# A fused attention and mixer kernel: the hand-written order of all steps up to the last block is replaced by another

## The chip, the cores and the metric

The kernel runs on one core of a Trainium2 chip. A core has five engines that each take their own instructions in order: TensorE (PE in the profile, with PEld for its weight loads), VectorE (DVE), ScalarE (ACT), GpSimd (POOL) and SyncE (SP). They meet only at semaphores. DMA transfers are issued by SyncE, GpSimd and ScalarE and land later. The metric is the device time of one execution in microseconds (us).

## The reference

Causal attention over 8 batches of 8 heads, 576 tokens and head size 64, with 16 extra "beacon" keys that every token sees; then a token mixer of low rank and a two-layer channel network, both with a residual.

```python
k_all = np.concatenate([beacon_k, k], axis=2)
v_all = np.concatenate([beacon_v, v], axis=2)
scores = scale * np.matmul(q, k_all.transpose(0, 1, 3, 2))
scores = np.where(causal, -1000000000.0, scores)
...
a = np.exp(scores)
a /= a.sum(-1, keepdims=True) + 1e-09
x = np.matmul(a, v_all)        # (8, 8, 576, 64) -> (8, 576, 512)
...
h = xt @ U @ V                 # xt: x with its last two axes swapped, rank 32
u = x + h.transpose(0, 2, 1)
out = u + np.maximum(u @ w_ch1, 0.0) @ w_ch2     # 512 -> 2048 -> 512
```

## The kernel before

Attention works on 32 pairs of heads, four pairs to a batch (pair p is batch p // 4). The mixer's result is one row of 8 x 576 = 4,608 tokens, and the channel network takes it in nine blocks of 512. Blocks 0 to 5 start with plain products against w_ch1 (step g) and use a Strassen-like scheme of seven half-size products for w_ch2 (step P); blocks 6 to 8 use such a scheme for both (F and P).

What stands where is written out by hand. One string, SCRIPT (L855), lists 961 steps, and a loop runs them one after the other; a step puts its instructions at the end of the queue of each engine that it uses. No scheduler reorders them. So the string sets the order on every engine at once, and a letter in a step's name can choose the engine of a copy (V for DVE, A for ACT). The steps that matter here:

- q, k, b, v and w: loads, all issued by GpSimd. The k and q of a batch go into staging tiles st0 and st1 (512 KB each, the main part) and hd0 and hd1 (the first 64 or 80 tokens, "heads", and the beacons). st0, st1, hd0 and hd1 have two buffers each.
- G: regroups one pair's q or k from st into the tile pr, on DVE or ACT.
- R: turns pr into raw with a DMA transpose on SyncE (L283, `turn_pair`), from pair 12 on. The heads of q and k are turned straight into qT and kT (L276, `turn_heads`).
- T: brings one pair's q or k into qT or kT. For pairs 0 to 11 it transposes on PE (L261, L263, tile tps) and copies; from pair 12 on it copies from raw (L291 or L109).
- S: one visit of the scores. Sa, Sb, Sc and Sd take the four groups of key columns of a pair: 496, 464, 496 and 208 query columns (L316, tile sps). The two heads of the pair have 64 rows each and use the two halves of the array side by side; each gets a PSUM bank, and ACT takes the exp of each (L321, tile expt).
- M masks on DVE; A multiplies the scores by v on PE (L331, tile po) and normalises on DVE.
- x and X: the turn of the attention's result and the token mixer. X.0 (L371) uses 32 columns of the array at a time, X.1 and X.2 (L397) 32 rows.
- g, p, P, U, F, V, N, W: the channel network. g is four matmuls of 512 columns (L529, tile gps), evicted by ACT, and for the lower half of them by DVE too. P is eight matmuls of 256 columns per step (L620, tiles cpY, cpA, cpD). U turns a block's input on SyncE (tile ut). N makes sums of w_ch1 (wf0 to wf3), which the last three blocks use.
- I: an idle matmul of 512 columns on the whole array that keeps PE busy; `S..:n` issues n of them ahead of a visit.

PSUM has eight banks, handed out in the order of the steps. Two places of the code decide what a moved step brings with it. The heads of a batch are turned along with a pair unless a lower pair of the batch has been turned already:

```python
    def turn_of(p):
        b, c = divmod(p, NH2)
        if not any(b * NH2 + i in raw_of for i in range(c)):
            turn_heads(Ls[b], qT_of(b), kTs[b % 2], c)
        raw_of[p] = turn_pair(prs[p])
```

And the sums of w_ch1 live in the staging buffers of k and q (two of each), from the step that makes them to the end:

```python
                first_sums[j] = stage.tile([P, H, 4 * D], F16, name=f"wf{j}", tag=f"st{j % 2}").rearrange(
```

The last 21 steps of the string, from P83's neighbours on, and everything behind them (a general path that these inputs don't take) belong to no part of the change.

Of the kernel before, what the change touches and what calls it, by code (L numbers as in the profile page):

```python
# [27 lines left out]
def kernel(  # L28
# [762 lines left out]
    def step(t):  # L791
# [69 lines left out]
        TkA7 X0.0 X0.1 Sa5:0 X0.2 Sb4 TqV7 TqV6 Sc5 TkA6 v1A g0.9 Sc4 M4.1 Sb5 M5.1 U0.0 U0.2 g0.13
        GkV11 g0.1 M5.0 g0.10 g0.0 GkV8 g0.14 q2 g0.3 g0.11 GkA9 A5.0 A5.1 Sb7 I1 w11 TkV8 GqV8 GqV9 Sa7
        g0.2 M4.0 GqV11 Sd7 Sc7 TkV11 TkA9 g0.8 A4.1 M7.0 TqA9 A4.0 p00.0 p00.1 Sb6 v1B Sa6:0 g0.12
        p00.2 TqV11 M7.1 Sc6 g0.4 Sd6 g0.15 M6.0 GkA10 w20 U0.1 M6.1 TqV8 g0.6 A7.1 A7.0 Sd9 Sc9 w21
        A6.1 g0.7 A6.0 Sd8 g0.5 Sc8 Sa8 GqV10 X1.0 v2 b3 p01.0 p01.2 X1.1 P02.0 p01.1 X1.2 W0 P01.0 Sb8
        W4 W5 W1 Sb9 Sa9 W2 U1.1 W6 P01.1 TkA10 P02.1 M8.1 M9.0 TqA10 W7 b4 M8.0 U0.3 P05.0 P05.1 q3
        P06.0 P06.1 M9.1 A8.1 A9.0 A8.0 Sa10 P03.0 P03.1 k3 g1.15 A9.1 q4 Sa11 Sd10 g1.5 g1.1 Sb10 Sc10
        g1.3 g1.2 GkV13 GqA12 M10.0 GkA12 W3 P07.0 M10.1 P07.1 GqA13 Sb11 Sd11 GqA14 Sc11 M11.1 g1.9
        M11.0 GkA14 g1.12 A10.0 g1.7 g1.10 g1.0 R12 R13 R14 g1.6 TkV12 TqV12 TkV13 P04.0 GqA16 A11.1
        g1.8 U1.0 U1.3 TqA13 GkA15 P04.1 g1.14 A11.0 k4 A10.1 Sa13 Sd12 g1.11 p10.0 g1.4 GqA17 g1.13  # L870
        Sa12 Sb12 Sc12 p11.0 GqV15 X2.0 M12.0 P11.0 GkA17 P11.1 U1.2 X2.1 GkV16 p11.1 R15 P12.0 P12.1
        R16 P16.0 TqV14 Sd13 Sb13 M12.1 p10.1 p10.2 Sc13 P16.1 b5 U2.2 M13.0 TkA14 v3 A12.1 q5 A12.0 R17
        GkA19 P15.0 P15.1 p11.2 Sa14 Sd14 Sc14 x12 P17.0 TkV15 M13.1 P13.0 U2.3 A13.0 Sb14 Z16 M14.0
        P17.1 P13.1 GqA19 GqA18 TkV16 TqA16 A13.1 g2.13 g2.10 TqV17 TqV15 M14.1 v4 g2.4 Sa15 k5 Sc15
        TkA17 P14.0 A14.0 P14.1 A14.1 Sd16 GqV20 Sb15 Sd15 M15.1 GkV18 g2.0 x14 Sc16 M15.0 g2.7 g2.5
        g2.2 A15.0 A15.1 x13 Sd17 Sb17 g2.9 U2.0 X3.0 b6 Sa16 X2.2 g2.3 x15 Sa17 Sb16 R18 R19 Z18 GkV20
        M16.1 Sc17 M17.1 M17.0 g2.1 g2.6 g2.12 M16.0 g2.8 g2.15 A17.0 U2.1 TqA19 GqA21 TqA18 X3.1 A16.1
        A17.1 g2.14 A16.0 X3.2 g2.11 p21.0 P21.0 P21.1 GqA23 GkA21 q6 TkA18 p20.0 P22.0 P22.1 TkA19 R20
        p21.1 p20.1 Sc18 Sb18 P26.0 P26.1 R21 Sc19 Sd18 Sa19 p21.2 P25.0 P25.1 GkV22 p20.2 I1 Sd19 Sa18
        M18.0 U3.0 Sb19 M19.0 P27.0 M18.1 M19.1 P23.0 GqV24 GqA22 TqV20 P27.1 x16 P23.1 g3.11 TqA21  # L880
        GkV23 TkV20 TkA21 R22 b7 A19.1 g3.7 A19.0 R23 g3.13 g3.8 g3.5 Sa21 Sb21 Sc21 P24.0 P24.1 A18.1
        A18.0 Sb20 U3.3 Sd21 Sa20 M21.1 M21.0 g3.3 g3.2 Sc20 Sd20 X4.0 g3.4 M20.0 k6 GkV24 M20.1 g3.15
        GqA26 N5 v5 TkV22 g3.12 A21.0 U3.1 A20.0 g3.10 N1 GkA26 g3.1 x17 q7 g3.0 A20.1 TqV22 TqA23 TkV23
        g3.6 g3.14 g3.9 p30.0 p30.2 A21.1 Sc23 GkV25 p31.0 Sb23 GqV25 Sa23 R24 p30.1 x18 P31.0 P31.1
        GkV27 P32.0 P32.1 TkA24 p31.1 Sc22 p31.2 U3.2 k7 Sd22 v6 Sa22 P36.0 P36.1 Sb22 x19 M22.1 Sd23
        M23.0 P35.0 R25 R26 M22.0 P35.1 X4.1 P37.0 P37.1 X4.2 GqV27 TqA24 TqA25 P33.0 U4.1 P33.1 TkA25
        P34.0 R27 g4.0 GqV28 A22.1 TkV26 GkA28 R28 M23.1 g4.11 GqV29 g4.2 g4.6 TqV26 A23.0 g4.10 A23.1
        Sd25 Sc25 A22.0 g4.4 GkV29 R29 Sb25 GkV30 Sa25 M25.0 Sd24 TqV27 P34.1 TkA27 g4.3 U4.3 TkV28
        M25.1 g4.15 g4.13 g4.9 Sc24 Sa24 x21 Sb24 M24.0 U4.2 X5.0 A25.0 M24.1 g4.8 g4.12 U4.0 GqV31 x22
        g4.1 p40.0 p40.1 GqA30 A25.1 g4.7 Sa27 Sb27 A24.1 g4.14 A24.0 g4.5 p41.0 GkV31 Sc27 x23 Sc26  # L890
        p41.2 p41.1 Sd26 P41.0 P41.1 Sa26 Sd27 M27.1 Sb26 P45.0 p40.2 P42.0 P42.1 P45.1 TkA29 x20 X5.1
        U5.3 A27.1 R30 TqV29 M27.0 P46.0 P46.1 P43.0 P43.1 g5.13 A27.0 M26.0 M26.1 Sd29 g5.11 X5.2 g5.4
        U5.1 TqV28 P47.0 g5.2 A26.1 TkA30 x27 P47.1 A26.0 N0 Sb29 Sc29 R31 N4 g5.6 N2 Sb28 Sa29 g5.0 x24
        P44.0 g5.15 TqA30 M29.1 P44.1 x25 Sd28 Sa28 v7 Sc28 M28.1 M28.0 A29.1 g5.7 g5.14 TkV31 g5.1 g5.5
        M29.0 A28.0 g5.3 N3 A28.1 Sb30 TqV31 Sa30 g5.10 A29.0 U5.0 g5.12 g5.9 x29 g5.8 N6 p51.0 p51.2
# [5 lines left out]
        p61.0 V8.0 P61.0 V7.3 F64.2 F64.1 F76.0 F76.3 U7.1 p61.1 U6.3 p60.0 p60.1 p60.2 U6.0 P61.1 P62.0
        P62.1 P65.0 p61.2 P65.1 guard V7.2 P66.0 P66.1 P63.0 P63.1 F75.3 F72.0 F72.3 F75.2 F77.0 F73.0
        P67.0 P67.1 F73.3 F71.1 F71.2 F72.1 F72.2 F76.1 F76.2 F75.1 V8.2 V8.1 P64.0 P64.1 F77.1 F77.2
        V8.3 F81.0 F74.0 F73.1 F74.1 U8.2 F77.3 p70.0 p70.2 F74.2 sum F73.2 p71.0 P71.0 p70.1 F74.3
        p71.2 F85.1 p71.1 F81.1 P71.1 P72.0 P72.1 F85.3 P75.0 P75.1 P76.0 P76.1 P73.0 P73.1 F82.1 U8.1
# [125 lines left out]
```

## Time and profile before

| | us |
|---|---|
| median of 3 runs | 339.44 (338.67 to 341.15) |
| the profiled execution | 339.2 |
| its span, first to last instruction | 337.5 |

| engine | busy us | share of the span | instructions |
|---|---|---|---|
| PE | 327.8 | 97% | 3527 |
| PEld | 228.0 | 68% | 3527 |
| DVE | 264.8 | 78% | 690 |
| ACT | 228.0 | 68% | 494 |
| POOL | 99.3 | 29% | 129 |

The span of the profile is 1.7 us shorter than the time of the same execution. The granted TensorE clock was 0.998. A busy share is an average over stages: the start, where scores and loads come in (to about 34 us), the long middle where attention of one batch runs beside the channel network of another (to about 240 us), and the blocks at the end. Matmuls are pipelined and their ends are modelled, so PE's rate is read from start times that follow each other, and not from the duration of a row.

### The profile page before, as it was taken

The numbers are of one execution on the slowest core, as the hardware profiler recorded it, in microseconds if no ns is written. First come the engines' busy times: TensorE is split into PE (matmuls) and PEld (weight loads), VectorE is DVE, ScalarE is ACT, GpSimd is POOL, SyncE is SP. The second block draws the span as 40 slices with busy tenths as digits, with TensorE's granted clock in tenths as the row PEclk, the third lists the DMA queues.
The fourth block names the chain that finished last, engine by engine and source line by source line (L and its number), as shares of the span: only waits on it lengthen the run. The fifth ranks groups of instructions, "written<-read, shape, count | busy, mean of one in ns | idle before, by whom it ended". The sixth has DMA issues, their size and how long they took to land.

```text
span 337.5 us, 8954 instructions
## 1 busy us (share of the span) xinstructions
PE 327.8 (97%) x3527; PEld 228.0 (68%) x3527; DVE 264.8 (78%) x690; ACT 228.0 (68%) x494; POOL 99.3 (29%) x129
## 2 busy tenths in 40 slices
...
GB/s 178 221 196 196 153 167 195 98 168 175 164 180 176 169 188 150 124 136 187 189 109 145 172 183 96 83 114 100 51 62 161 93 2 63 80 0 95 3 113 98
DMA packets 136145, 44.17 MB, mean 131 GB/s; under 512 B 108417, under 2 KB 131969, under 8 KB 136097
## 3 DMA queue, kind: packets, MB, share of 16 engines
q0 software_dynamic: 69008, 17.54, 61.3%
q1 hardware_dynamic: 66496, 25.66, 42.0%
...
q10 hardware_dynamic: 592, 0.34, 0.3%
...
## 4 chain that ended last, share of the span: by engine, by line
PE 75%; DVE 16%; DMA 3%; issue 3%; ACT 2%; SPq 0%; DVEq 0%; ACTq 0%
PE gps L529 23%; PE cpY L620 15%; PE po L331 8%; PE sps L316 8%; PE cpD L620 7%; PE cpA L620 3%; PE fpY L566 3%; DMA stm<-in_q_dram 3%; DVE gT L581 3%; DVE sT L601 2%; DVE ob L645 2%; DVE uT L404 2%; PE fpD L566 2%; PE tps L263 1%; ACT expt L321 1%
## 5 line engine op out<-in xcount | busy, mean ns | idle before, releaser
L321 ACT ACTIVATE expt<-sps 128x496 f16<-128x496 f32 (+2 forms) x256 | 111.6, 538 | 15.8 <-PE sps L316 14.3
L529 PE MATMUL gps<-uT,w 128*128 128x512 f16 x384 | 91.8, 379 | 0.0
L620 PEld LDWEIGHTS <-gT 128*128 128x128 f16 x576 | 54.6, 98 | 10.5 <-issue 2.2
L529 PEld LDWEIGHTS <-w 128*128 128x128 f16 x384 | 34.3, 98 | 37.4 <-issue 2.5
L587 POOL TENSOR_SCALAR gT<-gT 128x512 f16<-128x512 f16 x12 | 17.8, 1495 | 105.6 <-DVE gT L581 89.0
L620 PEld LDWEIGHTS <-sT 128*128 128x128 f16 x432 | 41.0, 98 | 7.8 <-issue 2.0
L331 PEld LDWEIGHTS <-expt 128*128 128x128 f16 (+1 forms) x960 | 35.5, 98 | 9.2 <-DVE expt L304 1.3
L203 POOL DMA_DIRECT2D vs<-in_v_dram x50 | 40.5, 825 | 3.2 <-DMA w<-in_moe_w_ch_dram 2.5
L539 ACT ACTIVATE gT<-gps 128x512 f16<-128x512 f32 x48 | 29.8, 630 | 15.5 <-PE gps L529 15.2
L304 DVE TENSOR_TENSOR expt<-expt,bigmask 128x512 f16<-128x512 f16 x64 | 26.7, 417 | 17.2 <-ACT expt L321 17.2
L331 PE MATMUL po<-vs,expt 128*128 128x65 f16 (+1 forms) x960 | 38.0, 194 | 1.0 <-ACT expt L321 1.0
L620 PE MATMUL cpY<-wsum,gT 128*128 128x256 f16 x288 | 36.1, 273 | 0.0
L620 PE MATMUL cpD<-w,sT 128*128 128x256 f16 x288 | 35.5, 273 | 0.3 <-DVE sT L601 0.3
L316 PE MATMUL sps<-qT,kT 64*128 64x80 f16 (+4 forms) x384 | 34.5, 282 | 0.4 <-ACT kT L109 0.3
L340 DVE TENSOR_TENSOR xb<-po,rec 128x320 f16<-128x320 f32 x64 | 31.5, 492 | 2.2
L534 DVE SCALAR_TENSOR_TENSOR gT<-gps,gT 128x256 f16<-128x256 f32 x48 | 19.8, 420 | 14.9 <-ACT gT L533 14.8
L109 ACT ACTIVATE hP<-fpY 128x512 f32<-128x512 f32 x24 | 13.7, 598 | 23.0 <-PE fpY L566 18.8
L533 ACT ACTIVATE gT<-gps 128x256 f16<-128x256 f32 x48 | 19.5, 418 | 11.5 <-PE gps L529 11.0
L316 PEld LDWEIGHTS <-kT 64*128 64x128 f16 x384 | 13.9, 94 | 18.7 <-issue 10.1
L645 DVE TENSOR_TENSOR ob<-cpY,ut 128x512 f32<-128x512 f32 (+1 forms) x28 | 18.7, 667 | 6.0 <-PE cpY L620 6.0
L566 PEld LDWEIGHTS <-wf 128*128 128x128 f16 x192 | 18.6, 98 | 3.0 <-issue 0.7
L620 PE MATMUL cpY<-w,gT 128*128 128x256 f16 x144 | 17.7, 273 | 0.0
...
## 6 DMA issues: line engine op xcount, KB each, us to landing
out_dram<-ob SPq DMA_DIRECT2D x16, 512.0 KB, 4.5
st<-in_k_dram POOLq DMA_DIRECT2D x6, 512.0 KB, 8.9
st<-in_q_dram POOLq DMA_DIRECT2D x6, 512.0 KB, 8.6
...
w<-in_moe_w_ch_dram POOLq DMA_DIRECT2D x4, 512.0 KB, 8.6
...
```

The costliest lines, as they stand in the source:

```text
L203: nc.gpsimd.dma_start(out=dst[a : a + nq[j], j, :, :], in_=src[hs, ds(q0[j], nq[j]), :].rearrange("h p d -> p h d"))
L304: nc.vector.tensor_tensor(out=e4, in0=e4, in1=bigmask, op=ALU.min)
L316: nc.tensor.matmul(ps[i][:, ds(o, w)], kT[hp, c, ds(P * ch, P)], qT[hp, c, ds(qa, w)], start=True, stop=True,)
L321: nc.scalar.activation(out=ex[i][:, ds(PAD + SLOT * g, gw[g])], in_=ps[i][:, 0 : gw[g]], func=AF.Exp, scale=scale)
L331: nc.tensor.matmul(po[:, j, :], ex[0 : nk[c], ds(blk[(c, j)], P)], vs[0 : nk[c], ds(c * H * E + h * E, E)], start=(c == 0), stop=(c == j),)
L340: nc.vector.tensor_tensor(out=xb[:, h // 2, :, ds(D * (h % 2), D)], in0=po[:, :, 0:D], in1=r.broadcast_to([P, NT, D]), op=ALU.mult)
L529: nc.tensor.matmul(g, w1[:, cc, ts(dc, P)], uT[:, cc, ds(ring(t0), 512)], start=(cc == 0), stop=(cc == NCC - 1))
L534: nc.vector.scalar_tensor_tensor(out=gT[:, dc, H2:512], in0=g[:, H2:512], scalar=0.0, in1=gT[:, dc, 0:H2], op0=ALU.max, op1=ALU.subtract,)
L539: nc.scalar.activation(out=gT[:, dc, :], in_=g, func=AF.Relu)
L566: nc.tensor.matmul(ps[:, i, :], a[:, kk, ts(2 * mp + i, P)], b[:, kk, :], start=opens and i == 0 and kk == 0, stop=kk == 1, skip_group_che ...
L620: nc.tensor.matmul(ps[:, i, :], a[:, f, ds(P * i, P)], b[:, f, :], start=opens and i == 0 and f == 0, stop=f == NK - 1, skip_group_check=True,
L645: nc.vector.tensor_tensor(out=out, in0=ps[:, ii, :], in1=other, op=ALU.add)
```

## The change

The string is replaced by another with the same 961 steps. Up to the last 21 the order differs; 61 steps of copying (H, G, T, e) also change their engine, in both directions. The loads keep their order among each other. The number of instructions on PE and of idle matmuls stays the same.

```diff
     SCRIPT = """
-        HqA0 I1 GkA0 I1 I1 I1 GqA0 I1 I1 HkV0 u I1 I1 I1 GkV1 I1 B I1 I1 I1 TqA0 TkA0 I1 TkV1 I1 s v0A
+        I1 I1 I1 GkV1 I1 I1 I1 HqA0 I1 HkA0 I1 GqA0 I1 I1 I1 I1 I1 v0A GkA0 v0B TqV0 TkV0 TkV1 I1 I1 Sa0:3
...
```

Three places show it. On PE, the score visits of pairs 8 and 9 beside the products of block 0. Here sps are scores (128x208 is visit d, 128x336 the first part of visit c), po is attention times v, gps is a product of block 0, and qtp is the mixer. Before:

```order
L331 MATMUL po_1268<-vs1_127,expt0_120 128x65
L316 LDWEIGHTS kT0_124
L316 MATMUL sps0_1286<-qT_989,kT0_124 128x208
L316 LDWEIGHTS kT0_124
L316 MATMUL sps1_1287<-qT_989,kT0_124 128x208
L529 LDWEIGHTS w1_108
L529 MATMUL gps_1292<-uT_118,w1_108 128x512
```

After:

```order
L371 MATMUL qtp_1279<-xb_934,Usb_111 32x128
L316 LDWEIGHTS kT0_124
L316 MATMUL sps0_1302<-qT_1036,kT0_124 128x208
L316 LDWEIGHTS kT0_124
L316 MATMUL sps1_1303<-qT_1036,kT0_124 128x208
L316 LDWEIGHTS kT0_124
L316 MATMUL sps0_1308<-qT_1036,kT0_124 128x336
```

Before, visit d of pair 8 stands alone between two groups of full-array matmuls; after, visit d of pair 9 is followed by visit c of pair 8 at once (and that by visit b of pair 9), and ahead of it stands a group of the mixer that uses a part of the array too. Over the program there are 68 unbroken stretches of score matmuls before and 56 after. Visits in one stretch number three in 21 of the stretches before and in 26 after.

On SyncE, the turns of batch 3 (hd1 and hd0 are its heads, raw its pairs; ut is a block's input, ob a result on its way out). Before:

```order
L650 DMA out_0_dram<-ob_1449 128x2x512
L276 DMA_TRANSPOSE qT_1800<-hd1_1346 128x4x64
L276 DMA_TRANSPOSE kT1_125<-hd0_1345 128x4x80
L283 DMA_TRANSPOSE raw_1803<-pr_1695 128x8x128
L283 DMA_TRANSPOSE raw_1805<-pr_1693 128x8x128
L283 DMA_TRANSPOSE raw_1807<-pr_1733 128x8x128
L520 DMA_TRANSPOSE ut_1438<-uT_118 128x4x128 x2
```

After:

```order
L276 DMA_TRANSPOSE qT_1721<-hd1_1349 128x2x64
L276 DMA_TRANSPOSE kT1_125<-hd0_1348 128x2x80
L283 DMA_TRANSPOSE raw_1724<-pr_1498 128x8x128
L276 DMA_TRANSPOSE qT_1721<-hd1_1349 128x3x64
L276 DMA_TRANSPOSE kT1_125<-hd0_1348 128x3x80
L283 DMA_TRANSPOSE raw_1760<-pr_1638 128x8x128
L276 DMA_TRANSPOSE qT_1721<-hd1_1349 128x4x64
L276 DMA_TRANSPOSE kT1_125<-hd0_1348 128x4x80
L283 DMA_TRANSPOSE raw_1779<-pr_1500 128x8x128
L650 DMA out_0_dram<-ob_1419 128x2x512
L520 DMA_TRANSPOSE ut_1439<-uT_118 128x4x128 x3
```

Pairs 12, 13, 14 were turned in rising order, with the heads once; now it is 14, 13, 12, each with the heads of its own and all higher pairs again. In the other batches pairs 17 and 16, 22 and 20, 25 and 24 change places like that, so head turns go from 10 to 20.

On DVE, the first sum of w_ch1 (wf0) and the copies from k's staging tile (st0; st0_1423 is batch 4's, st0_2556 batch 6's, st1_1424 is q's). Before:

```order
L253 COPY pr_2956<-st0_2556 128x512
L304 TENSOR_TENSOR expt1_121<-expt1_121,bigmask_107 128x4x128
L306 TENSOR_TENSOR expt1_121<-expt1_121,mask_102 80x80
L489 TENSOR_TENSOR wf0_3236<-w1_108 128x1024
L291 COPY kT1_125<-raw_2991 128x512
```

After:

```order
L645 TENSOR_TENSOR ob_1973<-cpD_2076,ob_1973 128x2x256
L489 TENSOR_TENSOR wf0_2228<-w1_108 128x1024
L534 SCALAR_TENSOR_TENSOR gT_2230<-gps_2231,gT_2230 128x256
L253 COPY pr_2238<-st1_1424 128x512
L645 TENSOR_TENSOR ob_1974<-cpY_1904,ob_1974 128x2x256
L304 TENSOR_TENSOR expt3_123<-expt3_123,bigmask_107 128x4x128
L306 TENSOR_TENSOR expt3_123<-expt3_123,mask_102 80x80
L253 COPY pr_2238<-st0_1423 128x512
```

The first sum moved from a place among batch 6's copies to one among batch 4's, so it takes one of k's two staging buffers two batches sooner.

More of the change, by code (lines that the diff above doesn't have):

```diff
@@ L861 @@
[L861 to L895, printed above, removed]
@@ L901 @@
[L901 to L905, printed above, removed]
@@ new lines @@
+        w12 A0.1 GqV3 I1 Sa1:2 b1 Sc1 I1 M1.1 A0.0 I1 TkV3 Sb2 Sc2 M1.0 GqV5 I1 I1 A1.1 TqV3 GqA4 Sd2 Sa2:1
+        I1 k1B I1 TqA5 I1 GkV5 A1.0 q1B Sb3 Sc3 I1 TqA4 M2.1 Sd3 Sa3:1 cV w13 A2.1 GkV4 b2 I1 I1 w10 M2.0
+        TkV4 k2 TkA5 A2.0 GkA7 I1 M3.1 I1 I1 v1A Sa4 Sb4 Sd4 M3.0 GqV6 A3.1 A3.0 eV I1 GkV6 Sa5:0 X0.0 Sd5
+        X0.2 Sc4 TqV6 GqA7 X0.1 Sc5 Sb5 M5.1 M4.0 GkV10 TkA7 TkV6 U0.2 M5.0 U0.1 g0.15 M4.1 q2 g0.11 TqV7
+        g0.3 w11 g0.0 U0.3 g0.8 g0.10 A4.0 A4.1 v1B Sa6:0 Sc6 A5.1 g0.2 GkA9 GqV10 GqV8 Sd6 Sb6 GqV9 TkA10
@@ new lines @@
+        w20 A5.0 M6.1 M6.0 GkV8 TkV9 U0.0 g0.1 g0.9 Sa7 Sc7 p00.0 g0.14 g0.12 TqA9 TqV8 TkV8 TqV10 g0.6 Sb7
+        Sd7 w21 g0.13 M7.1 M7.0 A6.0 g0.4 A7.1 GkA11 A7.0 A6.1 GqV11 g0.7 g0.5 X1.0 Sd9 Sc8 Sb9 p00.2 TkV11
+        v2 P01.0 b3 p01.0 p01.1 X1.1 X1.2 Sc9 p00.1 P01.1 b4 W0 W4 q3 P02.0 U1.2 Sa8 Sd8 W1 W5 W2 W6 P02.1
+        Sa9 Sb8 TqA11 P05.0 k3 p01.2 GqA14 GqA12 P05.1 M9.1 P06.0 P06.1 P03.0 P03.1 M9.0 M8.1 P07.0 q4 g1.0
+        W7 A9.0 k4 A8.1 g1.1 g1.2 M8.0 g1.11 g1.13 GkV13 P07.1 GkV14 W3 A8.0 A9.1 Sb11 Sd11 GqV13 g1.8 g1.3
@@ new lines @@
+        P04.0 R14 Sa10 Sc11 Sc10 g1.12 R13 GkV12 g1.4 g1.5 R12 g1.6 P04.1 g1.7 Sd10 Sa11 Sb10 M11.0 M11.1
+        g1.14 GqA16 M10.1 g1.10 TqA14 M10.0 TkA12 TqV13 A11.0 g1.9 U1.1 g1.15 b5 A10.1 p10.0 P11.0 A11.1
+        U1.0 GkV17 U1.3 TqA12 TkA14 v3 A10.0 GqA15 TkV13 p11.0 P11.1 GkV16 Sb12 Sc12 GqA17 R17 q5 Sa12
+        p10.1 p11.1 P12.0 P12.1 P16.0 Sd12 Sd13 X2.0 R16 M12.1 P15.0 M12.0 p11.2 p10.2 P16.1 Sc13 Sa13 Sb13
+        P15.1 GkV15 P17.0 M13.0 R15 X2.1 P13.0 A12.1 A12.0 U2.1 P13.1 N1 g2.0 GqV19 Sa14 Sb14 Sc14 TqA16
@@ new lines @@
+        U2.3 P17.1 TqA15 Z16 g2.12 g2.14 M13.1 GkV19 g2.1 g2.2 A13.0 TkA15 A13.1 TkV17 g2.7 Sd14 Sc15 GqA22
+        P14.0 Sd15 Sb15 Sa15 M14.1 GkV18 g2.11 M14.0 M15.1 R19 P14.1 v4 U2.0 g2.6 A14.0 k5 TqV17 g2.4 M15.0
+        A14.1 GqA18 x14 TkA16 b6 x12 g2.13 g2.5 g2.10 g2.15 GkV20 A15.1 Sd16 Sc16 Sb16 g2.9 A15.0 GkV22 R18
+        TqV19 U2.2 g2.8 g2.3 X2.2 X3.0 p21.0 x13 Sb17 Sa16 Sa17 p20.0 p20.1 GqV20 P21.0 Z18 q6 p21.1 P21.1
+        Sc17 Sd17 p20.2 TqA18 x15 M17.0 P22.0 GkV21 P25.0 TkA19 R22 M16.1 X3.2 R20 TkA18 p21.2 P25.1 P26.0
@@ new lines @@
+        P22.1 P26.1 b7 X3.1 A16.1 GqA21 R21 P23.0 P27.0 M16.0 P23.1 M17.1 g3.15 A17.0 GkA23 A16.0 Sc18 Sb18
+        Sa18 k6 v5 P27.1 g3.1 TkA20 TkV22 A17.1 TqA22 TkV21 Sd18 M18.1 GqV24 Sc19 M18.0 P24.0 g3.12 g3.6
+        GqV23 P24.1 TqA20 Sd19 Sa19 Sb19 A18.1 g3.10 GqV25 GkV24 A18.0 TqA21 M19.0 g3.9 g3.2 M19.1 R23 Sc20
+        GkA25 U3.1 N2 Sa20 Sd20 g3.5 g3.13 A19.0 g3.3 U3.3 A19.1 Sb20 Sd21 R25 M20.1 g3.7 M20.0 U3.0 TqV23
+        TkV23 x19 Sb21 Sa21 Sc21 M21.0 GqA27 GkV27 g3.8 A20.1 A20.0 g3.11 x16 M21.1 g3.0 g3.14 p30.0 x17
@@ new lines @@
+        g3.4 p31.0 Sb22 Sc22 X4.0 GqV26 p30.1 U3.2 A21.1 P31.0 P31.1 x18 A21.0 p30.2 p31.1 R24 Sa22 Sc23
+        Sd23 P36.0 P36.1 q7 Sd22 Sa23 Sb23 P35.0 M22.1 GkV26 R27 p31.2 P35.1 X4.2 M22.0 k7 M23.0 TkA24
+        P32.0 TqV25 P33.0 P37.0 X4.1 TkV25 M23.1 P32.1 R26 P33.1 v6 N5 A22.0 TqV24 g4.8 A23.0 g4.14 A23.1
+        g4.15 g4.1 P37.1 g4.11 A22.1 Sb24 Sa24 Sd25 P34.0 P34.1 GkV28 Sd24 Sb25 X5.0 Sc25 Sc24 Sa25 TkV26
+        M24.1 g4.13 GkV29 M25.0 g4.5 TkA27 U4.0 M25.1 g4.12 GqV28 M24.0 g4.10 U4.2 g4.6 g4.0 g4.9 g4.4
```

32 lines of the change are left out of this document (20 added, 12 removed).

## The prediction

> **What bounds the kernel now.** I read the busy time by stage first, then TensorE's waits, and then its instructions in order of time. The columns of the first are each engine's busy us in a stretch, with instruction counts.
>
> ```profile
> core 0: us, PE busy (x) PEld busy (x) DVE busy (x) ACT busy (x) POOL busy (x), PEclk, DMA share, GB/s
> 0.00:34.00 34.00, 29.85 (x354) 16.40 (x355) 24.35 (x103) 26.13 (x65) 24.42 (x43) 1.00 1.38 198
> 34.00:240.00 206.00, 205.96 (x2259) 132.10 (x2261) 159.03 (x432) 163.96 (x358) 57.03 (x74) 1.00 1.34 148
> 240.00:280.00 40.00, 39.66 (x451) 33.68 (x451) 38.54 (x84) 18.52 (x38) 6.05 (x4) 1.00 0.43 78
> 280.00:337.50 57.50, 52.33 (x474) 45.83 (x471) 42.89 (x74) 19.36 (x35) 11.75 (x8) 0.99 0.22 66
> PE idle L241 <- POOL ident masks.py:199: 1.6, 1, 1.6
> PE po L331 <- ACT expt L321: 1.0, 1, 1.0
> ```
>
> From 34 to 240 us TensorE (PE) has 205.96 busy us in 206.00: it waits for nobody there. VectorE (DVE) and ScalarE (ACT) are busy 77% and 80% of it. Only 240 to 280 has a second full engine, DVE with 38.54 of 40. So the order can change the time in two ways: PE's own work can get shorter, or a wait can be put in where now there is none. The removable waits are small: outside the 1.6 us at the very start the longest is 1.0.
>
> A busy PE is not yet a PE at its peak, so the second look is at start times of PE rows that follow each other.
>
> ```profile
> 143.48 0.38 PE L241 MATMUL idle<-ident 128*128 128x512 f16 x1
> 143.79 0.70 PE L316 MATMUL sps<-qT,kT 64*128 64x208 f16 x6
> 144.43 1.05 PE L620 MATMUL cpY<-wsum,gT 128*128 128x256 f16 x8
> 145.31 1.04 PE L620 MATMUL cpD<-w,sT 128*128 128x256 f16 x8
> ...
> 147.93 1.03 PE L529 MATMUL gps<-uT,w 128*128 128x512 f16 x4
> 148.79 0.63 PE L331 MATMUL po<-vs,expt 128*128 128x65 f16 x15
> 149.26 1.03 PE L529 MATMUL gps<-uT,w 128*128 128x512 f16 x4
> ...
> 204.26 1.03 PE L529 MATMUL gps<-uT,w 128*128 128x512 f16 x4
> 205.22 0.69 PE L316 MATMUL sps<-qT,kT 64*128 64x336 f16 x14
> ```
>
> Four gps matmuls followed by po, also a full-array matmul, take 148.79 - 147.93 = 0.86 us from start to start, 0.42 ns a column. The same four followed by a score (64 rows of the array, "64*128") take 205.22 - 204.26 = 0.96. **Entering a score stretch costs 0.10 us.** Leaving: the six score matmuls at 143.79 are three visits of 208, 496 and 464 columns, two heads side by side, so 1,168 columns or 0.49 us, and cpY starts 0.64 later. The 0.15 left over holds the exit and two steps from visit to visit; I take 0.10 for an exit, like an entry.
>
> **The change, part by part.**
>
> *Score stretches.* By the built order the 3,527 matmuls change the part of the array in use 177 times before and 148 after: score stretches go from 68 to 56 (24 changes), and the groups on 32 rows or columns now more often stand next to a score (5 more). 29 x 0.10 = 2.9 us, all on PE and so on the path. Bounds: 29 x 0.095 (entry seen behind the idle matmul: 0.31 us to the next start, less 0.215 for 512 columns) = 2.75, and 29 x 0.15 = 4.3 if the whole left-over belonged to the exit. I take 2.9; two clean entries stand behind it.
>
> The Trainium skill, TensorEngine Tiling (Array Packing), Key Properties, says that a change of tiling mode drains the engine. TensorE: Matmul & The Clock Gate, Step-by-step, puts a drain at about 128 cycles; at one column a cycle and the row's 0.42 ns that is an estimated 0.054 us, and the sum would be 1.6 us and not 2.9. The row shows more, and the row decides.
>
> *Idle matmuls.* The same 44 are issued (37 in steps of their own). Before, two stand behind the first gps row, one of them at 143.48; after, none does. Each holds a full PE for 0.215 us: -0.4. In the start they fill waits and cost nothing as long as those waits exist; without that cover they cost the 0.4 again.
>
> *Engines of copies.* Six copies from raw move from DVE to ACT, and others move back.
>
> ```profile
> L109 ACT ACTIVATE kT<-raw 128x512 f16<-128x512 f16 x10 | 11.2, 1128 | 0.0
> L109 ACT ACTIVATE pr<-st 128x512 f16<-128x512 f16 x24 | 15.0, 646 | 1.5 <-DMA raw<-pr 1.5
> L291 DVE COPY kT<-raw 128x512 f16<-128x512 f16 x10 | 6.1, 608 | 1.0 <-DMA raw<-pr 1.0
> L321 ACT ACTIVATE expt<-sps 128x496 f16<-128x496 f32 (+2 forms) x256 | 111.6, 538 | 15.8 <-PE sps L316 14.3
> ```
>
> ACT: +6 x 1.12, -6 x 0.63 (pr), and smaller ones, between +1 and +2 us of 228; DVE about even. PE hides it: ACT has 42 us free between 34 and 240. What is not hidden is a burst. An exp takes 111.6 / 256 = 0.44 us, so a stretch of three visits gives ACT 2.6 us of work in 0.6 us of PE. Before there are 21 such stretches, after 26; the 21 leave no PE wait in the rows from 34 to 240. I take 0.3 us; ends 0 and 3 (one PE wait of 0.6 for each of the five more).
>
> *Start.* qT and kT of pair 0 move from ACT to DVE, behind the copy of pair 1's k.
>
> ```profile
> 6.93 0.49 DVE L253 CAST pr<-stm 128x512 f16<-128x512 f32 x1 [0.83 <-DMA stm<-in_k_dram]
> 7.81 0.73 ACT L109 ACTIVATE kT<-tps 128x80 f16<-128x80 f16 x2
> 8.08 0.20 DVE L264 COPY kT<-tps 128x80 f16<-128x80 f16 x1
> 8.19 0.68 DVE L265 COPY kT<-tps 128x512 f16<-128x512 f16 x1
> 8.60 0.46 PE L316 MATMUL sps<-qT,kT 64*128 64x208 f16 x4 [0.34 <-ACT kT L109]
> 34.19 1.02 PE L529 MATMUL gps<-uT,w 128*128 128x512 f16 x4
> ```
>
> DVE is free of that copy at 7.42 and of its head copy (0.20) at 7.6; two times 0.78 (8.08 to 8.87) end at 9.2, so the first score starts near 9.2 and not at 8.60: +0.6. Later DVE has about 1.2 us more before the mix of batch 0. Against that PE gets all scores of pairs 4 and 5 done before the first gps, and PE is idle 34.00 - 29.85 = 4.15 us there, 1.6 of them before its first instruction, so 2.5 could still be won. Ends -2.5 and +1.8; I take +0.3, nearer to the later first score, which is certain.
>
> *SyncE.* Heads (L276) are now turned again for each pair that goes ahead of a lower one of its batch: ten issues become twenty, and each later one waits until the earlier one into the same tile has landed.
>
> ```profile
> L276 SPq DMA_TRANSPOSE qT<-hd x5: 1175/1185/1299, 74.3 to 187.4; - x5
> L276 SPq DMA_TRANSPOSE kT<-hd x5: 1186/1211/1292, 76.3 to 188.7; - x5
> DMA to landing us min/median/max: 2.3/7.3/10.3
> L283 SPq DMA_TRANSPOSE raw<-pr x20: 1232/1338/5233, 79.8 to 221.0; - x20
> raw<-pr SPq DMA_TRANSPOSE x20, 4.6
> ACT pr L109 <- DMA raw<-pr: 1.5, 1, 1.5
> POOL hd L193 <- PE tps L263: 8.7, 1, 8.7
> 33.37 31.16 SPq L520 DMA_TRANSPOSE ut<-uT  x5
> 73.75 0.41 SPq L650 DMA_DIRECT2D out_dram<-ob  x1
> ```
>
> Ten issues are 12 us more of SyncE's queue, and the outputs and the turns of ut and xt stand behind them. The worst place is pairs 14, 13, 12. From the first head turn to raw of pair 12 landed, before: 2 x 1.2 + 3 x 1.34 + 4.6 = 11 us. After: two rounds in which kT's turn is issued 1.2 behind qT's and then has to land, then 2.4, one raw and its landing, 2 x (1.2 + 7.3) + 2.4 + 1.3 + 4.6 = 25 at the median landing and 15 at the shortest. Behind the ACT copy that waits for it PE still has two g (0.86 each), two products (0.88 each, 144.43 to 145.31) and three po groups (0.47 each, 148.79 to 149.26), 4.9 us, before it needs ACT. The copies from raw wait 1.5 and 1.0 us at most now (ACT's above, DVE's in the copies' rows). The heads' loads stood 8.7 us behind the last transposes of batch 2, which for k now come some 7 us of PE work sooner, so fewer loads should be under way when the heads are turned. I take the shortest landing, 4 us more, which the 4.9 cover: 0.2 us. Ends 0 and 14 - 4.9 = 9.
>
> *Loads.* The four st buffers are two for k and two for q, and a sum of w1 (wf0) takes one of k's for good as soon as it is made. Before, that is behind k's load of batch 6; after, it is ahead of batch 5's, so k of batches 5 to 7 uses one buffer, and each load starts when the last copy of the batch before is done.
>
> ```profile
> POOL st L196 <- DVE pr L253: 24.4, 1, 24.4
> st<-in_k_dram POOLq DMA_DIRECT2D x6, 512.0 KB, 8.9
> ```
>
> Before, GpSimd waits like that once, for batch 7, and nobody on PE's side waits for it. After, 7.8 us of PE work stand between the last copy of batch 4's k and the first of batch 5's, 9.5 for batch 6, against 0.9 to issue and 8.9 to land: DVE is held up to 2.0 and 0.3 us, with GpSimd's later loads queued behind. PE's banks cover most of it: +0.5; ends 0 and 2.3.
>
> **Sum**, against the profiled execution (339.2; span 337.5 and 1.7 around it): -2.9 - 0.4 + 0.3 (bursts) + 0.3 (start) + 0.2 (turns) + 0.5 (loads) = -2.0, so 337.2. The median of the runs, 339.44, lies 0.2 above that execution: **337.4**. About 1% is what a measurement can tell from no change: 336.0 and 342.8.
>
> **Rivals.** (a) The start is won too: the first gps row comes 1.5 us sooner and the new waits are all covered: 339.4 - 2.9 - 0.4 - 1.5 + 0.4 = 335.0. For it: 2.5 idle us, and more scores ahead of the first gps; against it: the first score is later and DVE has more before the mix.
>
> (b) The repeated head turns hold ACT at pairs 14 to 12: with landings at the median 7.3, 14 us later than now, less 4 of lead (SyncE issues nothing from 64.5 to 73.75 and could run ahead by part of that) and 4.9 of cover, PE stands 5: 339.4 - 2.0 + 5 = 342.4, slower than before. It decides from a landing of 4.6 us on. For it: the median of 7.3; against it: the shortest of 2.3, and the sooner loads.
>
> (c) Banks: visits of a stretch take two of eight PSUM banks each, and PE stands behind the exps. At 0.6 us on each of the five added stretches of three it gives 3: 339.4 - 2.0 + 2.7 = 340.1. The Trainium skill, Perfetto Trace Analysis, Matmuls, asks that independent groups rotate through the banks so that evacuation overlaps the next matmuls; that speaks for this rival. Against it: the 21 stretches of three in the rows now.
>
> (d) The stretches save nothing, because the 0.10 would come back as waits of the same length for ACT: 339.4. The two entries, one behind gps and one behind an idle matmul that waits for nobody, speak against.
>
> **Chances.** The forecast 0.52, within 336.0 and 339.0; (a) 0.20; (b) 0.14; (c) 0.09; (d) 0.05. Range 334.8 to 341.6: it leaves out the far side of (a) and most of (b). Faster by over 1%: (a) and the edge of the forecast, 0.24. Slower by over 1%: the upper half of (b), 0.07. Within: 0.69.
>
> **What would show it.** Right: between 34 and 240 us the PE rows keep no idle time while the last gps rows come 2 to 3 us sooner; fewer, longer score rows; GpSimd waiting for pr at three k loads; L276 x10 each. Wrong: a wait of PE for ACT or DVE of over 2 us near 85 to 100 us (turns) or near 120 and 150 (loads); ACT waiting for raw by more than 5 us; a first gps row that has moved by more than 2 us either way.

## The result: 1.4% slower

The new kernel takes 343.55 us in the median of 4 runs (341.88 to 346.85), the one before 339.14: a ratio of 1.0141, with a 95% interval of 1.0097 to 1.0186. Forecast were 337.4, with 334.8 to 341.6. The profiled execution took 344.79 us, its span is 343.1; the rows below are from it, and it lies 1.2 us above the median. Ratios, here and below, leave out executions that were slow as a whole (two each of e3 and e6, one each of e7 and e12 below), and medians hold all of them.

First the busy time by stage of the new kernel. Before, TensorE (PE) was busy for 205.96 of the 206.00 us from 34 to 240.

```profile
core 0: us, PE busy (x) PEld busy (x) DVE busy (x) ACT busy (x) POOL busy (x), PEclk, DMA share, GB/s
34.00:240.00 206.00, 201.60 (x2207) 129.72 (x2204) 153.84 (x426) 157.18 (x342) 57.14 (x74) 1.00 1.38 150
...
90.00:100.00 10.00, 8.55 (x113) 6.30 (x112) 7.11 (x21) 10.00 (x18) 6.13 (x8) 1.00 1.92 149
...
112.00:120.00 8.00, 7.36 (x72) 4.21 (x70) 3.85 (x13) 8.00 (x17) 3.30 (x4) 1.00 1.73 159
...
150.00:165.00 15.00, 13.23 (x131) 7.40 (x130) 8.69 (x26) 13.21 (x29) 6.75 (x9) 1.00 1.82 182
```

PE now stands for 4.4 us in a stretch where it never stood, 3.9 of them in three places; in two of these ScalarE (ACT) is busy without a break. Next the rows of PE, ACT, VectorE (DVE) and SyncE (SPq) at these places in the timeline, each with what ended the idle time ahead of it:

```profile
95.12 1.15 ACT L109 ACTIVATE qT<-raw 128x512 f16<-128x512 f16 x1
...
96.33 0.51 PE L316 MATMUL sps<-qT,kT 64*128 64x464 f16 x4 [0.43 <-ACT qT L109]
...
99.41 0.69 DVE L645 TENSOR_TENSOR ob<-cpY,ut 128x512 f32<-128x512 f32 x1 [1.30 <-DMA ut<-uT]
...
100.16 0.38 PE L620 MATMUL cpY<-wsum,sT 128*128 128x256 f16 x2 [1.17 <-DVE ob L645]
...
114.10 2.08 ACT L109 ACTIVATE qT<-raw 128x512 f16<-128x512 f16 x2
...
117.52 1.14 ACT L109 ACTIVATE kT<-raw 128x512 f16<-128x512 f16 x1
...
118.72 0.39 PE L316 MATMUL sps<-qT,kT 64*128 64x336 f16 x6 [0.64 <-ACT kT L109]
...
145.43 1.17 SPq L276 DMA_TRANSPOSE qT<-hd  x1
146.69 1.20 SPq L276 DMA_TRANSPOSE kT<-hd  x1
148.00 2.77 SPq L283 DMA_TRANSPOSE raw<-pr  x2
...
153.11 1.09 ACT L109 ACTIVATE kT<-raw 128x512 f16<-128x512 f16 x1 [1.79 <-DMA raw<-pr]
...
155.47 2.03 PE L316 MATMUL sps<-qT,kT 64*128 64x208 f16 x6 [0.71 <-ACT expt L321]
...
157.88 0.62 PE L331 MATMUL po<-vs,expt 128*128 128x65 f16 x15 [0.38 <-DVE gT L534]
```

Two things are read here. At 95 and 118 the scores wait for a copy out of raw that ACT makes behind other copies. At 100 and 155 data is late: ut of a block, and raw of two pairs, whose turns SyncE issued at 148.0, behind a second turn of the same batch's heads. That second turn of qT's heads went out at 145.43, 0.02 us after the first one, issued at 136.73, had landed (145.41). The six score matmuls at 155.47 hold 0.49 us of columns and take 2.41 until the next kind starts.

To see where the time goes independently of the order, I counted for each PE row how far its start lies behind the work done so far: the columns of all matmuls ahead of it at 0.417 ns, two score matmuls side by side counted as one, four of the mixer's on 32 rows or columns as one, idle matmuls as nothing. The work is 286.6 us in each kernel. The table, worked out from the 3,527 PE rows of each profiled execution, gives that lag in us.

```
us of work done     60    90   110   140   200    end
before            27.0  30.2  32.7  35.2  40.8   46.2
new kernel        27.1  32.6  34.6  41.1  47.2   51.9
heads once (e1)   26.6  31.4  33.4  38.0  43.7   48.5
e1 + 6 copies(e5) 26.5  29.3  32.1  36.4  42.1   46.8
```

The new kernel loses 1.8 us more than before between 60 and 110 us of work (about 87 to 145 us of time), 4.0 more between 110 and 140, 0.5 more between 140 and 200, and from 200 on 0.7 less.

The saving that the forecast rests on is there. In the median row, a change of the used part of the array adds 0.098 us to the distance from start to start, in both kernels. Summed over the rows this is 17.8 us before and 14.8 after: 29 fewer changes, 3.0 us. So in the profiled executions other losses of 8.6 us stand against it (5.6 of longer span and the 3.0).

### The profile page after: what moved, and what is told of

The parts are those of the page before. It is cut to its first block, busy times and chain, and to the rows that moved or that the text cites. A ratio compares the mean times of both kernels' runs of the same rounds, so it can differ in the third digit from the quotient of the medians.

```text
span 343.1 us, 8958 instructions
## 1 busy us (share of the span) xinstructions
PE 329.9 (96%) x3527; PEld 228.2 (66%) x3527; DVE 262.7 (77%) x693; ACT 227.4 (66%) x491; POOL 100.1 (29%) x129
## 4 chain that ended last, share of the span: by engine, by line
PE 72%; ACT 9%; DMA 8%; DVE 5%; SPq 2%; issue 2%; POOL 0%; DVEq 0%; ACTq 0%
PE gps L529 18%; PE cpY L620 15%; PE cpD L620 8%; PE po L331 6%; PE sps L316 6%; PE fpY L566 5%; ACT expt L321 5%; PE cpA L620 4%; PE fpD L566 3%; DMA xt<-xb 3%; DMA ut<-uT 2%; DMA stm<-in_k_dram 2%; DMA raw<-pr 1%; ACT qT L109 1%; PE fpA L566 1%
## 5 line engine op out<-in xcount | busy, mean ns | idle before, releaser
L529 PEld LDWEIGHTS <-w 128*128 128x128 f16 x384 | 35.0, 98 | 37.9 <-issue 3.2
L534 DVE SCALAR_TENSOR_TENSOR gT<-gps,gT 128x256 f16<-128x256 f32 x48 | 19.6, 420 | 25.5 <-ACT gT L533 25.3
L316 PE MATMUL sps<-qT,kT 64*128 64x80 f16 (+4 forms) x384 | 35.5, 282 | 3.0 <-ACT expt L321 0.7
L533 ACT ACTIVATE gT<-gps 128x256 f16<-128x256 f32 x48 | 20.2, 439 | 18.0 <-PE gps L529 17.8
L620 PE MATMUL cpY<-wsum,sT 128*128 128x256 f16 x144 | 17.8, 273 | 1.2 <-DVE ob L645 1.2
```

The source lines that it names most:

```text
L316: nc.tensor.matmul(ps[i][:, ds(o, w)], kT[hp, c, ds(P * ch, P)], qT[hp, c, ds(qa, w)], start=True, stop=True,)
L529: nc.tensor.matmul(g, w1[:, cc, ts(dc, P)], uT[:, cc, ds(ring(t0), 512)], start=(cc == 0), stop=(cc == NCC - 1))
L533: nc.scalar.activation(out=gT[:, dc, 0:H2], in_=g[:, 0:H2], func=AF.Relu)
L534: nc.vector.scalar_tensor_tensor(out=gT[:, dc, H2:512], in0=g[:, H2:512], scalar=0.0, in1=gT[:, dc, 0:H2], op0=ALU.max, op1=ALU.subtract,)
L620: nc.tensor.matmul(ps[:, i, :], a[:, f, ds(P * i, P)], b[:, f, :], start=opens and i == 0 and f == 0, stop=f == NK - 1, skip_group_check=True,
```

## The experiments

The theories. 1: the repeated turns of heads hold SyncE, so raw and ut come late. 2: copies that changed to ACT make it late; going back to the old engines mends that. 3, formed after the first four runs: what is left is ACT's queue at a few places, exps of long score stretches and copies from raw behind them. The rival to all is that a joined stretch only moves the wait. "Heads once" means that SyncE turns the heads of a batch one time, as in the kernel before.

Medians, and ratios to the kernel before on the same chip with their 95% intervals:

| run | median, us | ratio |
|---|---|---|
| e1 heads once | 341.35 | 1.0068 (1.0041 to 1.0095) |
| e2 engines of before | 347.63 | 1.0236 (1.0198 to 1.0274) |
| e3 both | 344.45 | 1.0141 (1.0103 to 1.0179) |
| e4 before, seven joins | 342.65 | 1.0101 (1.0071 to 1.0130) |
| e5 heads once, six copies | 339.86 | 1.0005 (0.9983 to 1.0027) |
| e6 six copies | 346.28 | 1.0127 (1.0040 to 1.0215) |
| e7 before, heads twice | 348.29 | 1.0219 (1.0143 to 1.0295) |
| e8 e5, two steps changed | 340.37 | 1.0043 (1.0020 to 1.0067) |
| e9 before, three joins | 339.97 | 1.0026 (1.0009 to 1.0044) |
| e10 new start, old rest | 346.41 | 1.0224 (1.0204 to 1.0244) |
| e11 new start and end | 345.82 | 1.0210 (1.0183 to 1.0238) |
| e12 old, new end | 338.70 | 0.9990 (0.9976 to 1.0005) |

**e1: heads turned once.**

```diff
     def turn_of(p):
         b, c = divmod(p, NH2)
-        if not any(b * NH2 + i in raw_of for i in range(c)):
-            turn_heads(Ls[b], qT_of(b), kTs[b % 2], c)
+        if not any(b * NH2 + i in raw_of for i in range(NH2)):
+            low = min(int(t[1:]) for t in SCRIPT.split() if t[0] == "R" and int(t[1:]) // NH2 == b)
+            turn_heads(Ls[b], qT_of(b), kTs[b % 2], low % NH2)
```

> The new kernel with one edit: the heads of a batch are turned once, at the batch's first R step, for all of its pairs that SyncE turns (10 head turns instead of 20); order and engines stay. In the new kernel TensorE's start-to-start rows hold some 6 us more waiting than before from 93 to 181 us: at 95.6, 98.7, 117.8 and 154 to 158. Theory 1 (the head turns that are repeated hold SyncE, so raw and ut land late): the waits of ScalarE and VectorE for raw (6.9 and 2.6 us) fall to under 3 together, the waits of TensorE at 117.8 and at 154 to 158 go, and the time is 338.5 to 340.5. Theory 2 (the copies from raw that moved to ScalarE make bursts that TensorE stands behind): the time stays within 342 and 344, and the waits stay.

It took 341.35, between the two: the ratio falls from 1.0141 to 1.0068, some 2.5 us, and the runs lie within 341.1 and 341.7 where the new kernel's spread over 5 us. In its trace ACT waits 2.1 us for raw and DVE no more; the wait for ut is gone. The scores that stood at 155 are down to 1.33 us from 2.41. The waits at 95 (0.5) and 117 (0.85) stay, though theory 1 had the second of them go. ACT's waits for raw in the new kernel, and then in e1:

```profile
ACT kT L109 <- DMA raw<-pr: 6.9, 2, 5.1
ACT kT L109 <- DMA raw<-pr: 2.1, 1, 2.1
```

Theory 1 holds, for about half of the slowdown; by the two intervals the 2.5 us is known to within some 1.8. Turning the heads once also gains from e2 to e3 (1.0236 to 1.0141) and from e6 to e5 (1.0127 to 1.0005).

**e7: the same cause put into the kernel before.**

```diff
-        if not any(b * NH2 + i in raw_of for i in range(c)):
+        if sum(b * NH2 + i in raw_of for i in range(NH2)) < 2:
             turn_heads(Ls[b], qT_of(b), kTs[b % 2], c)
```

> The kernel before, with the heads turned again at the second R step of each batch (10 head turns instead of 5, as many repeats as the new kernel has, in the order before). Theory 1 (a second turn waits until the first has landed, 9 to 10 us here, and holds raw of the next pairs and ut behind it): raw of pairs 13 and 14 lands some 5 us later, near 94 to 96 us, TensorE shows waits there and the time is 340.5 to 342. Rival (SyncE has the time, and the order before needs these raw tiles later): within 338.5 to 339.7.

It is slower than the new kernel: 343.6 to 352.4, all above what theory 1 gave. SyncE's rows of its profiled execution (352.4, the longest of the four), and PE's and ACT's:

```profile
73.43 1.20 SPq L276 DMA_TRANSPOSE qT<-hd  x1
75.91 1.26 SPq L276 DMA_TRANSPOSE kT<-hd  x1
79.01 1.39 SPq L283 DMA_TRANSPOSE raw<-pr  x1
82.86 1.18 SPq L276 DMA_TRANSPOSE qT<-hd  x1
86.48 1.17 SPq L276 DMA_TRANSPOSE kT<-hd  x1
87.75 2.63 SPq L283 DMA_TRANSPOSE raw<-pr  x2
...
92.68 1.13 ACT L109 ACTIVATE qT<-raw 128x512 f16<-128x512 f16 x1 [2.97 <-DMA raw<-pr]
...
93.86 0.74 PE L316 MATMUL sps<-qT,kT 64*128 64x496 f16 x4 [3.45 <-ACT qT L109]
```

The first turns landed at 82.84 and 86.46, 9.4 and 10.6 us after their issue, and only then the second ones go, at 82.86 and 86.48. Raw of pair 13 is issued at 87.75 and no longer at 81.28, lands at 92.66, and PE stands 3.45 us for it. The chain is the one that rival (b) described; where it strikes depends on the order. In this execution it strikes once more: ACT waits 8.46 us, up to 193.60, for a raw that was issued behind the second head turns of batch 6, and PE stands 4.09 us behind ACT and DVE.

**e2, e3: the engines of before.** Copies of pairs 12 to 31 get the letter that they had, 41 steps; e3 with e1's edit.

```diff
-GkV14 GqV13 GkV12 TqA14 TkA12 TqV13 TqA12
+GkA14 GqA13 GkA12 TqV14 TkV12 TqA13 TqV12
```

> The new kernel in its order, but each copy of pairs 12 to 31 (into pr, and from raw) runs on the engine that it had before: 41 tokens change their letter. Theory 2 (bursts of ScalarE): ScalarE is no longer busy through 90 to 100 us, the waits at 95.6 and 117.8 go and those at 154 to 158 get shorter, and the time is 339 to 341. Theory 1 (repeated head turns): raw still lands late at 108 and 153 us, and the time is 342 to 344.

> Both edits together in the new order: heads turned once for each batch, copies of pairs 12 to 31 on the engines of before. If the two causes together hold all of the 6 us of added waits, the time is the sum that was forecast, 336.5 to 338, with 148 changes of the array's part and hardly a wait of TensorE from 34 to 240 us. If a third cause is there (the order of the copies itself, or the loads with one buffer for k), it stays above 339.5.

Theory 2 falls as far as it speaks of all 41 copies: e2 is slower than the new kernel, and than either theory said. e3 stays above 339.5, the outcome named for a third cause. The edit also moves copies into pr to ACT's queue, from which the turns start, and the block's results wait for ut: DVE stood for ut 5.7 us in the profiled execution of e3 (349.36, five above its median). Order and engines are one choice; the old engines don't fit the new order.

**e4, e9: stretches joined in the kernel before.** Seven joins, or three of them; nothing else moves. Two of the seven:

```diff
-Sc6 g0.4 Sd6
+Sc6 Sd6 g0.4
-Sd8 g0.5 Sc8 Sa8
+Sd8 Sc8 Sa8 g0.5
```

> The kernel before with score stretches joined at seven places (one to four steps of TensorE set behind or ahead of the scores between which they stood) and nothing else moved: the built order has 62 score stretches instead of 68, and 166 changes of the array's part instead of 177. At 0.10 us for each change: 1.1 us less, 338.0 to 338.3. If a change saved comes back as a wait for ScalarE's exp: no difference, and TensorE's rows show waits inside the joined stretches.

> The kernel before with three of the seven joins of e4: those after which a stretch has three visits at most and no g stands behind its exps. 171 changes of the array's part instead of 177. If a join costs only where it makes a stretch of more than three visits or puts g behind the exps: no new wait, 0.6 us less in TensorE's rows, 338.3 to 338.9 (too little for the runs to tell). If any join gives its change back: TensorE's rows show waits of the same size, 339 to 339.6.

Both are slower than the kernel before, by 1.0% and 0.3%, though the changes fell by 11 and 6. The trace of e4 shows how, behind the second join of the diff. Its rows in the timeline, PE, then ACT, then DVE:

```profile
56.29 0.71 PE L316 MATMUL sps<-qT,kT 64*128 64x208 f16 x10
56.94 1.02 PE L529 MATMUL gps<-uT,w 128*128 128x512 f16 x4
...
60.32 0.28 PE L397 MATMUL ups<-Vsb,qts 32*128 32x240 f16 x4 [1.44 <-DVE qts L377]
...
56.64 2.48 ACT L321 ACTIVATE expt<-sps 128x208 f16<-128x208 f32 x6 [0.32 <-PE sps L316]
58.97 0.44 ACT L533 ACTIVATE gT<-gps 128x256 f16<-128x256 f32 x1
...
59.44 0.42 DVE L534 SCALAR_TENSOR_TENSOR gT<-gps,gT 128x256 f16<-128x256 f32 x1 [1.92 <-ACT gT L533]
...
59.98 0.28 DVE L377 CAST qts<-qtp 128x128 f16<-128x128 f32 x1
```

Ten score matmuls take PE 0.65 us and leave six exps, 2.48 us. The half of g that ACT makes (L533) comes behind them, DVE waits 1.92 for it, the small cast qts (L377) stands behind DVE's half, and the mixer's matmuls on PE wait 1.44. In the kernel before, the same cast began at 58.74: 1.24 earlier. The saving of a join was 0.2. Another join made a stretch of five visits, and there the banks themselves held PE (the same view, ACT and then PE):

```profile
75.12 4.34 ACT L321 ACTIVATE expt<-sps 128x496 f16<-128x496 f32 x10 [0.22 <-PE sps L316]
...
75.75 0.77 PE L316 MATMUL sps<-qT,kT 64*128 64x464 f16 x3 [0.42 <-ACT expt L321]
```

In e9 I had left such joins out; still three visits in one stretch held the next gps 0.42 us for a bank, and a mixer's matmuls stood 0.39 for xb, which DVE made late. Its joins save 0.6 and lose more: the second of the outcomes stated, and a little beyond it.

**e5, e6: six copies from ACT to DVE.** The six that stood in ACT's queue ahead of a wait of PE; e5 with e1's edit, e6 without.

```diff
-TqA14 GqA17 TqA15 TkA20 TqA22 TqA20
+TqV14 GqV17 TqV15 TkV20 TqV22 TqV20
```

> The new kernel with heads turned once, and six copies given to VectorE that ScalarE made (qT of pairs 14, 15, 20 and 22 and kT of pair 20 from raw, pr of q of pair 17), the ones that stand in ScalarE's queue ahead of what TensorE waits for at 95.1 (0.5 us), 99.4 (0.6), 116.6 (0.85) and 153.5 to 159 us (1.7 with the waits inside stretches) in the run with heads once. Theory 3 (what is left of the loss is ScalarE standing behind its exps and copies at these places): the four go, 3 us or more, and the time is 337.5 to 338.6. Rival (VectorE is just as late there, since its rows wait for ScalarE's halves of g, or the banks hold the scores): 340.5 to 342.

> The new kernel as it is, head turns repeated, with the same six copies on VectorE. If the two causes add up (turns 2.2 us, ScalarE's queue 3): 340 to 341, with raw still landing late at 108 and 153 us and ScalarE no longer the one that TensorE waits for at 95 and 117. If the late raw alone makes ScalarE late, so that the copies' engine is of no account: 343 to 344.

e5 is even with the kernel before, between the two outcomes stated; the waits at 95, 99 and 117 are gone from its trace. That at 153 stayed (1.08 us) and has another reason now, DVE's row for g behind five copies, as the rival said. PE's longest waits, leaving out the one ahead of its first instruction:

```profile
PE po L331 <- DVE gT L534: 1.1, 1, 1.1
PE sps L316 <- DVE qT L265: 0.7, 1, 0.7
```

e6 shows no gain of the six copies without the once-turned heads (1.0127 beside 1.0141), where a sum of two causes would have given 340 to 341; its interval is wide, and its median of 346.28 lies beyond both outcomes. In the profiled execution (349.66, the longest; runs from 341.25) PE stands for results that wait for ut, 3.5 and 2.8 us.

**e8: two steps more.**

```diff
-TqV22
+TqA22
-R18 TqV19 U2.2
+R18 TqV19 x15 U2.2
-TqA18 x15 M17.0
+TqA18 M17.0
```

> Heads once and the copies of e5 on VectorE but one: qT of pair 22 goes back to ScalarE, which waited for scores there while VectorE's row for g stood behind five copies (TensorE waited 1.1 us at 152.6); and the turn of xb of pair 15 goes one place ahead in SyncE's queue, in front of a turn of ut (VectorE waited 0.9 us for xt at 138.7, TensorE 0.9 behind it). If these are the places: 1 to 1.7 us less than e5, 338.0 to 338.8, a little faster than before. If the queue only moves the wait: 339.5 to 340.5.

The time is the one stated for a wait that only moves. The wait at 152 shrank from 1.1 to 0.2 in the profiled execution (342.59, 2.2 above the median), so that half was read rightly. The other was not: the last turn of xb was issued at 131.82, 0.9 us sooner than in e5, and landed at 140.37, 1.8 later, since it took 8.55 us and not 5.83. DVE waited 4.2 us for xt in all, not 1.5. In that execution the landing decided, and not the place in SyncE's queue.

**e10, e11, e12: the orders cut together.** Steps of one order up to a cut, then all others in the other order.

> The new order up to its first R step (265 of the 961 steps, to about 75 us), and the order before from there on: each step not yet done follows in the old order, copies of the rest on the engines of before. 160 changes of the array's part (before 177, new 148), heads turned 5 times two. In the traces the new start is ahead by some 0.4 us of TensorE's lag where this cut lies (runs with waits there alike), in spite of 1 us of later start. If the loss of the new order is all in its middle, as theories 1 and 3 have it, this keeps the start's gain and loses nothing: 338 to 338.8. If the start only borrows (copies put off that come due later): 339.3 or more, with new waits of TensorE between 75 and 130 us.

> As the run with the new start, and the new order once more from behind the last g of the sixth block (about 236 us) on; the middle is the old order. From there to the end the new kernel's TensorE rows lose 0.7 us less than before (the waits of 0.50 and 0.65 us near 275 and 282 us are gone, one of 0.57 is new). If parts add up: 337.3 to 338.2, faster than both. If not: no less than the run with the new start alone.

> The order before up to the last g of the sixth block (742 of the 961 steps, to about 240 us), and the new order for what is left from there on; 177 changes of the array's part as before. The traces show the new kernel losing 0.7 us less than before on this stretch, and the run with both ends new 0.5 us less: the waits of 0.50 and 0.65 us near 275 and 282 us go, one of 0.57 comes. If that stands alone: 338.3 to 338.6, 0.5 us less, which the runs can hardly tell; the trace tells it by the rows. If this cut, like the first one, leaves steps that come due late: a new wait of TensorE behind 236 us and 339.5 or more.

The start borrows. At 50 us of work e10 is 1.1 us ahead of the kernel before (lag 25.5 and 26.6), and at 70 it is 5.5 behind: the copy of pair 12 into pr waits in ACT's queue, behind exps of scores that now come sooner, until 86.51 (before, such copies ran from 78.62 on), SyncE turns the first pair at 87.28 and not at 79.84, and PE waits 3.4 us for qT. e11, with the new end as well, is no faster within the intervals than e10: the second of the outcomes stated.

The new end stands alone. From 200 us of work on the lag grows by 5.3 to 5.4 us in all five profiled executions with the old end (the kernel before, e4, e7, e9, e10), by 4.9 with the new end behind the old middle (e11, e12) and by 4.7 in the other seven. That is 0.4 to 0.7 us less, with 14 changes of the array's part there in each of them, so it is no saving of the stretches. e12's 338.70 can't be told from the kernel before (339.04 there).

## Why the prediction was wrong

**Score stretches, -2.9: right.** 3.0 by the rows. An entry costs 0.10, an exit 0.11, and from visit to visit 0.003. The left-over of 0.15 was read off an odd row: of twelve stretches of six score matmuls in the kernel before that no wait touches, the other eleven leave 0.11. The page of the Trainium skill that I set beside it, TensorEngine Tiling (Array Packing), Key Properties, gives no time for the drain, and the estimate of 0.054 us each from the other page was too small by half.

**Turns, +0.2: the step that failed first.** The term was mis-sized, and its place was wrong. I took the shortest landing, 2.3, since fewer loads should be under way. The first turns at 72 us landed after 7.7 and 6.8, near the median of 7.3 that I had set aside. With the median the sum was rival (b)'s 342.4, and the runs price the repeats at 2.5 us (new kernel to e1). That the median comes near is in part luck, for the place was another. At pairs 14 to 12 nobody waited for raw: the last of it landed at 90.80 in both kernels, and ACT began to copy it at 92.19; what was late there was ut, queued behind (1.17 on PE): issued at 91.16, 1.3 us later than in e1, and landed 8.1 us after that and not 4.5. The wait for raw that PE feels is at pairs 20 and 21, where the second head turn waited for the first (136.73 to 145.43); ACT's longest wait for raw, 5.1 at 188, leaves PE no wait of over 0.3. I had costed one place of the four, and by the earliest need of raw alone.

**Bursts, +0.3: mis-sized.** e5 less e1 is 0.6%, 2.1 us, for six copies. I hid ACT's added copies behind its 42 free us from 34 to 240, an average: ACT's busy time over the whole program did not even rise (228.0 to 227.4), but from 90 to 100 and from 112 to 120 it had nothing free. And I reasoned that 21 stretches of three (20 by the rows, and 26 after) left no wait before, so five more should leave little. But the joins of e4 and e9, new ones at other places, left waits. There the price of a burst was set by what stood next in ACT's and DVE's queues, which a count of stretches does not tell. Rival (c) came nearer in size with 3 us; its cause, the banks, is shown for the joins of e4 and e9, and in the new kernel at 155 alone, where ACT's exps stood behind late raw.

**Start, +0.3, and idle matmuls, -0.4: wrong together.** By 60 us of work 21 of the 29 changes are already saved, 2.1 us, and yet the lag is 27.1 against 27.0. So the start costs about 2.2 (1.7 in e1's execution) and not 0.3 less 0.4; the upper end was 1.8. Most of it has come by the first gps row, which is later by 1.2 us (35.34) though 9 changes fewer stand ahead of it. PE's idle time up to 34 us is about the same; what makes up the loss stays open.

**Loads, +0.5: nothing.** GpSimd does wait at more loads, as said:

```profile
POOL st L196 <- DVE pr L253: 9.9, 2, 6.0
POOL st L196 <- ACT pr L109: 3.5, 1, 3.5
```

but no row of DVE or ACT waits for st of k, so none of the delay reaches PE.

**The signs.** Named as signs of being wrong were waits of PE of over 2 us near 85 to 100 and 150, where all waits together came to 1.45 and 1.77, and ACT waiting for raw by over 5 us, which came to 6.9. The last gps row, forecast 2 to 3 us sooner, starts at 244.92 and not at 239.63. By the ratios the new kernel lies 4.8 us above the one before, 6.8 above the forecast of -2.0. Taken in the order of e1 and e5, the turns are 2.5 of them and ACT's six copies 2.1; in the order of e6 and e5 they are 0.5 for the copies and 4.1 for the turns, so only the 4.6 of both together, which is the slowdown itself, is independent of the order. The last 2.2 are what e5 still lacks to the forecast. Beside the changes saved, its rows lose some 1.6 in the start, up to 60 us of work, and 2.6 between 60 and 200. That this is of the same kind as the other losses is not shown.

## What to carry to other kernels

A saving on a full engine is real only as far as the engines that serve it stay on time: price each regrouping by what then stands behind the burst in every other queue, down to the next thing that the full engine needs. In these runs a turn that is repeated into the same tile went out only when the first one had landed, with all that is queued behind it; take the median landing under the load of that place, and look at each place. And where a schedule has no waits, its order and its choice of engines hold each other up: of another one's parts, the new start put in by itself cost 2.2%, and the new end nothing.

## What the runs showed of the chip

In these runs a long wait of PE cost more than its length. The busy time by stage of e7 and then of e2 around their waits:

```profile
90.20:93.70 3.50, 0.21 (x7) 0.18 (x4) 0.98 (x3) 1.02 (x1) 3.50 (x5) 1.00 1.38 132
93.70:95.00 1.30, 1.03 (x5) 0.41 (x5) 1.27 (x4) 1.30 (x4) 1.03 (x2) 0.59 2.55 150
95.00:97.10 2.10, 2.10 (x6) 0.73 (x5) 0.87 (x3) 1.72 (x5) 0.00 (x0) 0.50 2.41 134
```

```profile
98.80:101.40 2.60, 0.34 (x4) 0.16 (x2) 0.72 (x2) 1.52 (x4) 0.61 (x1) 1.00 2.22 136
101.40:103.30 1.90, 1.88 (x28) 1.17 (x31) 1.90 (x4) 0.43 (x2) 0.00 (x0) 0.72 2.04 138
103.30:105.50 2.20, 2.20 (x26) 1.44 (x15) 1.86 (x8) 0.62 (x3) 0.00 (x0) 0.50 1.46 179
```

The column after POOL is the granted clock. It falls to a half after the wait, for 3.4 us (93.9 to 97.3 in e7, 102.2 to 105.6 in e2), which is 1.6 us more in each case (the stretches by one less the clock). In such a stretch of e8 eight matmuls of 256 columns took 1.71 us from start to start, and 0.88 elsewhere. In e2 an idle time of 2.28 us was enough; single waits of 1.17 in the new kernel's profiled execution and of 1.66 in e6's did not do it. The Trainium skill, TensorE: Matmul & The Clock Gate, What's actually happening, has the clock halved after an idle window of about 3.4 us; here the shorter wait sufficed. It goes with the scatter of kernels that have such waits: e7's executions took 343.59 us at a mean clock of 1.000, 348.15 and 348.43 at 0.990, and 352.40 at 0.984, and the lost clock (one less the clock, times the span) is 3.5, 3.5 and 5.6 us of that. It is not all of the scatter: in e3, 349.88 us at 0.995 stands beside 344.45 at 1.000, and the clock makes 1.7 of that.
